# Scores on quarters of the TensorE array, transposes on the whole of it

## The chip, the cores and the metric

The kernel runs on one NeuronCore of a Trainium2 chip. The metric is the device time of one execution in microseconds; the kernel before takes 481.77 us (median of three runs, 481.53 to 481.87). In the profile PE is TensorE's matrix product, PEld its loading of weights, DVE is VectorE, ACT is ScalarE, POOL is GpSimd and SP is SyncE, which issues most transfers.

## What is computed

Two blocks follow each other. The first is a gated linear recurrence over 768 tokens for 4 batches x 8 heads, with a head of 48 values. For each token:

```
state = alpha[t][:, None] * state + outer(k[t], v[t])
y[t]  = q[t] @ state
```

The 8 heads of a token are put side by side into a row `x` of 384 values, 3072 rows in all. The second block is a feed-forward network without a nonlinearity: `((x @ w1) * (x @ w2)) @ w3 @ w_out`, with w1 and w2 of 384 x 1024, w3 of 1024 x 1024 and w_out of 1024 x 384. The weights arrive in double precision and are converted on the chip.

## The kernel before

**Part one, the recurrence, in 24 chunks.** A chunk is 128 tokens of one batch with all 8 heads; six chunks make up a batch. Inside a chunk the recurrence is turned into matrix products. `logs` and `decays` form the running product of the alphas (a logarithm, a triangular matmul, two exponentials) and `decayed` multiplies q and k by it, into `qk`, which has tokens on the partitions and each head padded from 48 to 64. Then four kinds of small products follow:

- `transposed(n)` (line 310) turns q and k of chunk n, so that the head's 48 values lie on partitions: two heads share the 128 partitions, the even one at 0 to 47 and the odd one at 64 to 111. ScalarE copies the two PSUM banks of results to `qkT` (line 312).
- `scores(n)` (line 350) multiplies k by q for each of the 8 heads, contracting over 48 values, to a 128 x 128 block. VectorE masks the two banks of results into `ms` (line 353).
- `attend_state(n)` (line 370) multiplies the state carried from the chunk before by q, and `attend(n)` (line 376) adds the masked scores times v. In the first chunk of a batch there is no state, and line 370 is left out.
- `outer(n)` (line 322) forms k times v, which VectorE and GpSimd add into the state. The last chunk of a batch leaves it out.

**Part two, the network.** Line 406 is the matmul of all its products, always the whole 128 x 128 array against 384 columns. The "gates" are the products with w1 and w2; part of them is handed out in pieces to the steps of part one, to fill TensorE. w3 and w_out are first multiplied with each other ("fold"), for which w3 is transposed on the whole array in line 508; at the end `project` multiplies the gates by the result.

**The order.** The loop at line 584 runs over n = 0 to 24, here called steps. A step loads inputs, then calls `attend_state(n - 1)`, `scores(n)`, `transposed(n + 1)`, `attend(n - 1)`, `outer(n)`, then pieces of gates and `decays(n + 3)` between them (line 275; line 272 in early chunks). `pieces` (line 598) is 0 up to step 6; after that every fourth step (10, 14, 18, 22) has none and the others have 3, 3 and 2. Before a step without pieces there is also a new group of x to be split in three (lines 398 to 400). Each engine works through its instructions in a fixed order that is settled when the kernel is built, and that follows this order of calls except for small exchanges. All PSUM tiles come from one pool of 8 banks, handed out in turn.

**How a small product lies on the array.** The partitions that its operands occupy choose the rows of the array, and the partitions of its result the columns. Before the change there are four shapes. Line 370 uses 64 x 64 quarters. Lines 350 and 310 use 64 rows x 128 columns, i.e. two halves. Lines 376 and 322 use 128 rows x 64 columns. The gates and line 275 use the whole array. An fp32 matmul appears in the profile as two instructions, a transpose as one.

Of the kernel before, what the change touches and what calls it, by code (L numbers as in the profile page):

```python
# [48 lines left out]
def kernel(  # L49
# [12 lines left out]
    nc = tc.nc  # L62
    B, H, S, D = q.shape
# [5 lines left out]
    NP = H // 2  # L69
    DP = 64  # L70
# [32 lines left out]
    def bank():  # L103
        return ps.tile([C, 512], FP32, tag="bank", name="bank")

    st, mark = {}, {}

    def after_marks(*names):
        stack = ExitStack()
        for x in names:  # L110
            stack.enter_context(tc.issue_after(mark[x]))
        return stack
# [16 lines left out]
    def load_a(n):  # L129
        if n < N:  # L130
            st["a", n] = inp.tile([C, H, D], FP32, tag="ac", name="ac")
            nc.sync.dma_start(out=st["a", n], in_=rows(alpha, n))

    def load_kq(n):
        if n >= N:
            return
        st["kq", n] = inp.tile([C, 2, H, D], FP32, tag="kq", name="kq")
        nc.sync.dma_start(out=st["kq", n][:, 0], in_=rows(k, n))
        nc.sync.dma_start(out=st["kq", n][:, 1], in_=rows(q, n))  # L139

    def load_v(n):
        if n < N:
            st["v", n] = vs[n % len(vs)]
            nc.sync.dma_start(out=st["v", n][:, :, 0:D], in_=rows(v, n))
# [10 lines left out]
    ident = const.tile([C, C], FP32, name="ident")  # L155
# [71 lines left out]
    def convert(steps, ahead=3):  # L227

        for _ in range(steps):
            fetch(ahead)  # L230
            if not begun:
                return
            x = begun.popleft()
            try:
                next(x)
                begun.appendleft(x)
            except StopIteration:
                pass
# [4 lines left out]
    def store():  # L243

        while later:
            dst, src = later.popleft()
            nc.sync.dma_start(out=dst, in_=src)

    def last(n):
        return n % NCH == NCH - 1  # L250

    def logs(n):
        if n >= N:
            return
        a = st.pop(("a", n)).rearrange("p h d -> p (h d)")
        la = st["la", n] = work.tile([C, DM], FP32, tag="la", name="la")
        nc.scalar.activation(la, a, AF.Ln)
        if n >= LATE:

            t = st["la", n] = work.tile([C, 2, DM], FP32R, tag="la2", name="la2", bufs=1)  # L260
            nc.scalar.copy(t[:, 0], la)
            nc.vector.tensor_sub(t[:, 1], la, t[:, 0].bitcast(FP32))
        if n in ends:
            nc.gpsimd.dma_start(out=ends[n][2:3], in_=a[0:1])
# [21 lines left out]
    def decayed(n):  # L286
        if n < N:
            mark["qk", n] = nc.vector.tensor_mul(qks[n % 3][:, :, :, 0:D], st.pop(("kq", n)),  # L288
                                 st.pop(("e", n)).rearrange("p i (h d) -> p i h d", h=H)).ins
# [9 lines left out]
    def transposed(n):  # L299
        if n >= N:  # L300
            return
        qk = qks[n % 3]
        qkT = work.tile([C, 2, NP, C], FP32, tag="qkT", name="qkT")

        tp = [bank().rearrange("p (i j c) -> p i j c", i=2, j=NP) for _ in range(2)]
        for i in range(2):
            for j in range(NP):
                for half in range(2):
                    s = ds(DP * half, DP)
                    nc.tensor.transpose(tp[half][:, i, j, :], qk[s, i, 2 * j:2 * j + 2, :], ident[s, s])  # L310
        for half in range(2):
            mark["qkT", n] = nc.scalar.copy(qkT[:, :, :, ds(DP * half, DP)], tp[half]).ins  # L312
        st["qkT", n] = qkT

    def outer(n):
        if n >= N or last(n):
            return
        qk, vc = qks[n % 3], st["v", n]
        s1 = bank()[:, 0:NP * D].rearrange("p (j d) -> p j d", j=NP)
        for j in range(NP):  # L320
            for i in range(2):
                nc.tensor.matmul(s1[ds(DP * i, DP), j, :], qk[:, 0, 2 * j + i, :], vc[:, 2 * j + i, 0:D],
                                 start=True, stop=True)

        if n % 2:
            to = st["T", n] = work.tile([C, NP, D], FP32, tag="tmp", name="tmp")
        else:
            to = Ts[1][:, :, 0:D]
        if n % NCH == 0:
            nc.vector.tensor_copy(out=to, in_=s1)  # L330
        else:
            nc.vector.tensor_add(to, s1, Ts[n % 2][:, :, 0:D])
# [11 lines left out]
    def scores(n):  # L344
        qkT = st["qkT", n]
        sc = [bank().rearrange("p (j c) -> p j c", j=NP) for _ in range(2)]
        for j in range(NP):
            for i in range(2):
                r = ds(DP * i, D)
                nc.tensor.matmul(sc[i][:, j, :], qkT[r, 0, j, :], qkT[r, 1, j, :], start=True, stop=True)  # L350
        ms = work.tile([C, 2, NP, C], FP32, tag="ms", name="ms")
        for i in range(2):
            masked = nc.vector.tensor_tensor(ms[:, i].bitcast(I32), sc[i].bitcast(I32), keep_bc, op=ALU.bitwise_and)  # L353
        ends_of_part1[0] = mark["ms", n] = masked.ins
        st["ms", n] = ms
# [3 lines left out]
    def attend_state(n):  # L359
        qkT = st.pop(("qkT", n))  # L360

        y = [bank()[:, 0:HP * C].rearrange("p (j c) -> p j c", c=C) for _ in range(2)]
        st["y", n] = y, [(half * HP + j, i, y[i][ds(DP * half, DP), j, :])
                         for j in range(HP) for i in range(2) for half in range(2)]
        if n % NCH:
            for j, i, to in st["y", n][1]:
                r = ds(DP * i, D)
                nc.tensor.matmul(to, Ts[n % 2][r, j, :], qkT[r, 1, j, :],  # L370
                                 start=(j % HP == 0), stop=False, skip_group_check=True)
# [22 lines left out]
    def split_x(g, i):  # L394
        x = st.pop(("xT", g))
        t = tr[i].tile([C, 3, KM, TG], FP32R, tag="x3", name="x3")
        st["x3", g] = t
        nc.scalar.activation(t[:, 0], x, AF.Copy, scale=1.0 - 2.0 ** -13)
        nc.vector.tensor_sub(t[:, 1], x, t[:, 0].bitcast(FP32))  # L399
        nc.vector.scalar_tensor_tensor(t[:, 2], t[:, 0].bitcast(FP32), -1.0 - 1.0 / P, x,  # L400
                                       op0=ALU.mult, op1=ALU.add)
# [73 lines left out]
    def gate(g, f):  # L475
        yield from (late_gate if late else early_gate)(g, f)
# [73 lines left out]
    def run(pieces):  # L550

        for _ in range(pieces):
            if not fill:
                return
            try:
                next(fill[0])
            except StopIteration:
                fill.popleft()
# [25 lines left out]
    for n in range(N + 1):  # L584
        store()
        load_v(n + AHEAD - 1)
        load_a(n + 5)
        load_kq(n + AHEAD)
        if n:
            attend_state(n - 1)  # L590
        if n < N:
            scores(n)
        transposed(n + 1)
        if n - 2 in begin:
            g, tiles = begin[n - 2]
            split_x(g, 0)
            fill.extend(gate(g, f) for f in tiles)
        pieces = (0, 3, 3, 2)[(n - 6) % 4] if n > 5 else 0
        if n == 0:
            with after_marks(("qkT", 0)):  # L600
                logs(2)
            decays(2)
            with after_marks(("e", 2)):
                logs(3)
        early = n < 7
        behind = after_marks(("qkT", n + 1), ("qk", n + 1)) if early else ExitStack()
        if n < N - 2:
            with behind:
                convert(2 if n == 0 else 1, 2 if n == 0 else 3)
        advance(n)  # L610
        if n:
            attend(n - 1)
        outer(n)
        run(pieces > 0)
        if early:
            with after_marks(("qkT", n + 1), ("qk", n + 1)):
                convert(1)
        with after_marks(*[("ms", n)] * (n < 3)):
            decayed(n + 2)
        logs(n + 4)  # L620
        if n in begin:
            load_x(begin[n][0])
        convert(early and n > 2)
        run(pieces > 1)
        decays(n + 3)
        if n < N - 2:
            convert(early or n % 3 == 0)
        run(pieces > 2)
        if n == N - 3:
            while begun:  # L630
                convert(1)
            weights.extend(load_out(j) for j in range(KF))
            fetch(4)
# [91 lines left out]
```

## Time and profile before

| Engine | Busy, us (share of 479.8 us) | Instructions |
|---|---|---|
| PE | 458.3 (96%) | 3824 |
| PEld | 434.4 (91%) | 3824 |
| DVE | 359.7 (75%) | 582 |
| ACT | 279.2 (58%) | 550 |
| POOL | 75.0 (16%) | 138 |

A busy share is a mean over stages. Part one lasts until about 190 us; after that PE runs matmuls of line 406 and the fold's transposes almost without a break. Since matmuls overlap each other, the mean duration of one (300 ns, say) is not what it costs. What it costs is the distance from one start to the next, and that is read from a timeline or from the chain of waits, where each piece covers only the time that it added.

### The profile page before, as it was taken

What the parts mean: (1) busy time and instruction counts of PE and PEld (TensorE: products, weight loads), DVE (VectorE), ACT (ScalarE), POOL (GpSimd) and SP (SyncE); (2) the same over time, 40 slices, a digit from 0 to 9 for tenths busy, and PEclk for the clock granted to TensorE, in tenths of its full rate; (3) what the DMA queues carried; (4) which work ended last, traced back from release to release, by engine and by line L of the source; (5) the groups of instructions that cost most, each with busy time, mean ns of one, the idle gap of its engine ahead of it and who ended that gap; (6) DMA issues with size and microseconds to landing.
All of it is one profiled execution on the core that took longest, in us unless ns stands there. A gap on an engine that the chain in (4) does not pass through costs nothing.

```text
span 479.8 us, 9999 instructions
## 1 busy us (share of the span) xinstructions
PE 458.3 (96%) x3824; PEld 434.4 (91%) x3824; DVE 359.7 (75%) x582; ACT 279.2 (58%) x550; POOL 75.0 (16%) x138
## 2 busy tenths in 40 slices
PE   4889889999998999999999999999999999999997
PEld 2576679899898998999999999999999999999996
DVE  2679999987989666999999788745541966667771
ACT  4566677766777454899777576545544533333330
POOL 2323132112201210112321112111111100000000
PEclk9998799999999999999999999999999999999999
DMA  9999999999999973557775443022104965556511
GB/s 157 192 198 203 219 216 192 219 210 216 214 215 226 217 222 110 190 158 246 227 215 188 135 159 100 34 100 83 49 34 132 258 193 167 169 172 179 180 51 49
DMA packets 155311, 80.29 MB, mean 167 GB/s; under 512 B 104672, under 2 KB 145760, under 8 KB 155264
## 3 DMA queue, kind: packets, MB, share of 16 engines
q1 hardware_dynamic: 149744, 65.23, 55.9%
q0 software_dynamic: 5520, 14.43, 9.2%
q8 instruction: 30, 0.49, 0.5%
q14 instruction: 17, 0.14, 0.1%
HBM read 57.58 MB, written 22.06 MB: 166 GB/s over the span
## 4 chain that ended last, share of the span: by engine, by line
PE 76%; DVE 8%; DMA 7%; ACT 3%; issue 3%; SPq 2%; ACTq 0%; DVEq 0%
PE bank L406 66%; DMA xT<-xd 2%; PE bank L376 2%; DMA raw<-in_moe_w_dram 2%; PE bank L350 2%; DMA ac<-in_alpha_dram 1%; PE bank L508 1%; PE bank L310 1%; DMA xd<-x 1%; DVE qk L288 1%; DVE ms L353 1%; PE bank L272 1%; DVE power L205 1%; DVE x L399 1%; SPq L139 1%
## 5 line engine op out<-in xcount | busy, mean ns | idle before, releaser
L406 PE MATMUL bank<-x,w 128*128 128x384 f32 x1152 | 211.2, 338 | 0.3 <-DVE x L400 0.3
L406 PEld LDWEIGHTS bank<-x,w 128*128 128x128 f32 x1152 | 200.1, 188 | 2.0 <-issue 1.3
L406 PE MATMUL bank<-w3o,ab 128*128 128x384 f32 x576 | 100.2, 336 | 0.0
L406 PEld LDWEIGHTS bank<-w3o,ab 128*128 128x128 f32 x576 | 99.9, 188 | 0.0
L431 ACT ACTIVATE bank<-bank 128x384 f32<-128x384 f32 x98 | 46.8, 477 | 42.7 <-PE bank L406 42.4
L415 ACT ACTIVATE t<-bank 128x384 f32<-128x384 f32 x62 | 30.4, 492 | 59.4 <-PE bank L406 59.1
L481 POOL DMA_DIRECT2D abd<-ab x46 | 27.5, 598 | 132.2 <-DVE ab L467 124.6
L467 DVE TENSOR_TENSOR ab<-bank,r 128x384 f32<-128x384 f32 x45 | 25.0, 555 | 22.7 <-ACT bank L431 17.7
L537 DVE TENSOR_TENSOR ab<-abl,ab 128x1024 fp32r<-128x1024 f32 x24 | 29.4, 1224 | 13.7 <-ACT ab L536 13.7
L536 ACT ACTIVATE ab<-abl 128x1024 fp32r<-128x1024 f32 x24 | 25.5, 1061 | 20.9 <-PE bank L406 18.9
L350 PEld LDWEIGHTS bank<-qkT 48*128 48x128 f32 x384 | 26.1, 204 | 10.8 <-issue 4.4
L406 PE MATMUL bank<-wo,w3T 128*128 128x384 f32 x192 | 35.9, 334 | 0.0
L350 PE MATMUL bank<-qkT 48*128 48x128 f32 x384 | 31.1, 304 | 3.7 <-DVE ms L353 2.4
L353 DVE TENSOR_TENSOR ms<-bank,keep 128x512 int32<-128x512 int32 x48 | 31.1, 686 | 4.2 <-PE bank L350 4.2
L406 PEld LDWEIGHTS bank<-wo,w3T 128*128 128x128 f32 x192 | 33.5, 188 | 0.0
L312 ACT COPY qkT<-bank 128x512 f32<-128x512 f32 x48 | 26.2, 591 | 11.0 <-PE bank L310 11.0
L417 DVE SCALAR_TENSOR_TENSOR o<-bank,t 128x384 f32<-128x384 f32 x24 | 13.4, 558 | 23.7 <-issue 15.2
L202 ACT ACTIVATE power<-power,rebias 128x512 uint32<-128x512 uint32 (+1 forms) x36 | 25.1, 699 | 9.0 <-DVE power L201 8.8
L197 ACT ACTIVATE rest<-raw 128x512 f32<-128x512 uint32 (+1 forms) x36 | 23.2, 647 | 12.0 <-DMA raw<-in_moe_w_dram 10.7
L288 DVE TENSOR_TENSOR qk<-kq,e 128x768 f32<-128x768 f32 x24 | 22.9, 954 | 8.9 <-ACT e L279 8.8
L538 DVE SCALAR_TENSOR_TENSOR ab<-ab,abl 128x1024 fp32r<-128x1024 f32 x24 | 29.2, 1219 | 0.0
L376 PE MATMUL bank<-ms,v 128*64 128x128 f32 x384 | 29.0, 294 | 0.0
(75 smaller groups left out, 571.6 us busy)
## 6 DMA issues: line engine op xcount, KB each, us to landing
abl<-abd SPq DMA_DIRECT2D x24, 512.0 KB, 4.5
abd<-ab POOLq DMA_DIRECT2D x46, 192.0 KB, 3.3
raw<-in_moe_w_dram SPq DMA_DIRECT2D x16, 512.0 KB, 5.1
raw<-in_moe_w_dram SPq DMA_DIRECT2D x24, 256.0 KB, 5.0
xT<-xd POOLq DMA_DIRECT2D x9, 576.0 KB, 4.6
ac<-in_alpha_dram SPq DMA_DIRECT2D x24, 192.0 KB, 5.3
kq<-in_k_dram SPq DMA_DIRECT2D x24, 192.0 KB, 5.3
kq<-in_q_dram SPq DMA_DIRECT2D x24, 192.0 KB, 4.3
```

Source lines behind the costliest of these rows:

```text
L288: mark["qk", n] = nc.vector.tensor_mul(qks[n % 3][:, :, :, 0:D], st.pop(("kq", n)), st.pop(("e", n)).rearrange("p i (h d) -> p i h d", h=H ...
L312: mark["qkT", n] = nc.scalar.copy(qkT[:, :, :, ds(DP * half, DP)], tp[half]).ins
L350: nc.tensor.matmul(sc[i][:, j, :], qkT[r, 0, j, :], qkT[r, 1, j, :], start=True, stop=True)
L353: masked = nc.vector.tensor_tensor(ms[:, i].bitcast(I32), sc[i].bitcast(I32), keep_bc, op=ALU.bitwise_and)
L376: nc.tensor.matmul(to, vc[:, 2 * j + i, :], ms[:, i, j, :], start=(n % NCH == 0 and j % HP == 0), stop=(j % HP == HP - 1), skip_group_chec ...
L406: nc.tensor.matmul(p, w[part][i], x[part][i], start=start and part == parts[0] and i == 0, stop=stop and part == parts[-1] and i == n - 1, ...
L415: nc.scalar.activation(t, p1, AF.Copy, scale=(1.0 + 1.0 / P) * scale)
L431: nc.scalar.activation(p, p, AF.Copy, scale=1.0 + 1.0 / P)
L481: (nc.gpsimd if late else nc.sync).dma_start(out=abd[g][:, f, :], in_=ab)
L536: nc.scalar.activation(t[:, 0], ab, AF.Copy, scale=1.0 - 2.0 ** -13)
L537: nc.vector.tensor_sub(t[:, 1], ab, t[:, 0].bitcast(FP32))
L538: nc.vector.scalar_tensor_tensor(t[:, 2], t[:, 0].bitcast(FP32), -1.0 - 1.0 / P, ab, op0=ALU.mult, op1=ALU.add)
```

## The change

Scores and transposes trade shapes. Each head's scores are split in two matmuls of 64 result rows each, so that they run on the quarters, as the state products just ahead of them do: 16 matmuls per chunk in place of 8. The transposes, 16 per chunk on 64 x 64 blocks before, become 8 on whole 128 x 128 blocks; ScalarE's two copies then take one bank for k and one for q, where each bank held one half of the tokens of both. In steps that have gates, the transposes move from behind the scores to behind the outer products, where the gates, also on the whole array, come next. The aim is fewer changes of shape on the array.

```
     def transposed(n):
-        tp = [bank().rearrange("p (i j c) -> p i j c", i=2, j=NP) for _ in range(2)]
         for i in range(2):
+            tp = bank().rearrange("p (j c) -> p j c", j=NP)
             for j in range(NP):
-                for half in range(2):
-                    s = ds(DP * half, DP)
-                    nc.tensor.transpose(tp[half][:, i, j, :], qk[s, i, 2 * j:2 * j + 2, :], ident[s, s])
-        for half in range(2):
-            mark["qkT", n] = nc.scalar.copy(qkT[:, :, :, ds(DP * half, DP)], tp[half]).ins
+                nc.tensor.transpose(tp[:, j, :], qk[:, i, 2 * j:2 * j + 2, :], ident)
+            mark["qkT", n] = nc.scalar.copy(qkT[:, i], tp).ins
...
     def scores(n):
         for j in range(NP):
             for i in range(2):
-                r = ds(DP * i, D)
-                nc.tensor.matmul(sc[i][:, j, :], qkT[r, 0, j, :], qkT[r, 1, j, :], start=True, stop=True)
+                for half in range(2):
+                    r, s = ds(DP * i, D), ds(DP * half, DP)
+                    nc.tensor.matmul(sc[i][s, j, :], qkT[r, 0, j, s], qkT[r, 1, j, :], start=True, stop=True)
...
             scores(n)
-        transposed(n + 1)
+        pieces = (0, 3, 3, 2)[(n - 6) % 4] if n > 5 else 0
+        if not pieces:
+            transposed(n + 1)
...
         outer(n)
+        if pieces:
+            transposed(n + 1)
         run(pieces > 0)
```

More of the change, by code (lines that the diff above doesn't have):

```diff
@@ L597 @@
             fill.extend(gate(g, f) for f in tiles)
-        pieces = (0, 3, 3, 2)[(n - 6) % 4] if n > 5 else 0
         if n == 0:
```

## The prediction

> **What bounds the kernel now.** I read the busy shares by slices first (40 slices of 12 us; digits are tenths).
>
> ```profile
> PE   4889889999998999999999999999999999999997
> ...
> DVE  2679999987989666999999788745541966667771
> ...
> PEclk9998799999999999999999999999999999999999
> DMA  9999999999999973557775443022104965556511
> ```
>
> PE is full from the seventh slice on. Before that VectorE and the transfers are as full as PE, and the clock dips. Next, what PE waits for between 65 and 190 us (in total, times, longest):
>
> ```profile
> PE bank L350 <- DVE ms L353: 1.7, 2, 1.3
> PE bank L275 <- ACT la L261: 1.0, 1, 1.0
> PE bank L310 <- ACT e L279: 0.7, 1, 0.7
> ```
>
> With two smaller rows (0.3 and 0.2) that is 3.9 us of 125. After 190 us there is no wait worth naming and nothing in the change. So from 65 us on the price of the change is PE time, less what those few waits can give back. Then the timeline of one step with gates (n = 16: start, length):
>
> ```profile
> 129.22 1.72 PE L406 MATMUL bank<-x,w 128*128 128x384 f32 x9
> 130.87 0.67 PE L370 MATMUL bank<-qkT,T 48*64 48x128 f32 x16
> 131.47 1.16 PE L350 MATMUL bank<-qkT 48*128 48x128 f32 x16
> 132.46 0.66 PE L310 MATMUL bank<-ident,qk 64*128 64x64 f32 x16
> 133.05 1.09 PE L376 MATMUL bank<-ms,v 128*64 128x128 f32 x16
> 133.97 0.62 PE L322 MATMUL bank<-v,qk 128*64 128x48 f32 x16
> ```
>
> The reader subtracts starts. State products take 0.60 us, scores 0.99, transposes 0.59, attends 0.92, and no group waits. These contain the cost of changing shape. Narrower windows give starts inside a group, and so the undisturbed spacing: state products start in fours 0.11 apart (131.03, 131.14), scores in pairs (131.68 for the second, so 0.78 / 7 = 0.11), transposes in pairs 0.06 apart. What exceeds that is the change of shape:
>
> - state to scores: the last four states start at 131.25, so the second pair of scores is due at 131.47 and starts at 131.68: **0.21 us**;
> - transposes to attends: second pair due at 133.06, starts at 133.21: **0.15**;
> - gates to state, read likewise: 0.15. Outer products to gates: second gate due at 134.60, starts at 134.81: **0.21**;
> - scores to transposes, and attends to outer, are of one shape: nothing;
> - state directly to attends, only in step 24 (188.59 for the last four, second pair due at 188.81, starts at 188.97): **0.16**.
>
> The row for a whole-array transpose is line 508; the chain of waits gives its net time, with gates around it:
>
> ```profile
> 253.83 0.87 PE bank L508 x8
> 254.71 13.53 PE bank L406 x78
> ```
>
> 0.87 / 8 = 0.109 us for one. Gates run at 13.53 / 78 = 0.173 behind them as everywhere, so whole-array transposes beside gates pay no change of shape.
>
> **What the Trainium skill says.** TensorEngine Tiling (Array Packing), Key Properties: changing the tiling mode, not only the tile, drains TensorE. The trace agrees: 0.15 to 0.21 us at each change and none within a mode. The same section says that different tiles load and multiply in parallel; the fours of line 370 start 7 ns or so apart within 0.03 us, so a quarter of the work per instruction is not a quarter of the speed. Restrictions on that page: column tiling excludes transpose mode for fp32. That is why the transposes cannot join the quarters and must take halves by rows or the whole array; no run so far shows it. TensorE: Matmul & The Clock Gate, Part 1: a little-used PE is put to half clock. The trace shows it early on: the stretch 51.7 to 58.5 us has a granted clock of 0.50.
>
> **The change part by part**, for a step in full clock.
>
> *Scores on quarters.* 32 passes in fours, 8 x 0.109 = 0.87 us, for 8 pairs, 8 x 0.111 = 0.89. Saves 0.02. No VectorE work changes: it masks the same two banks.
>
> *Transposes on the whole array.* 8 x 0.109 = 0.87 for 8 pairs x 0.062 = 0.50: **adds 0.37** in each chunk. The two 128 x 512 copies to `qkT` stay the same size (591 ns each in the groups view), and the first can begin when half the transposes are done; ScalarE has room (58% busy), so I cost it at nothing. Copies wait behind the later transposes in gated steps, but `qkT` is needed only in the next step, with 3 to 5 us of gates in between.
>
> *Changes of shape.* (a) Step with gates and state: before gates-state 0.15, state-scores 0.21, transposes-attends 0.15, outer-gates 0.21. After: gates-state 0.15, scores-attends 0.16 (as state-attends), outer-transposes 0.21 (as outer-gates), transposes-gates 0. Saves 0.20. (b) Step with gates, no state: there was no 0.21 in the middle to save; the first change falls from about 0.20 to 0.15: saves about 0.05. (c) Step without gates: the order stays, so quarters-transposes and transposes-attends replace 0.21 and 0.15. Neither is in the trace (quarters to whole, whole to column halves); bounded by 0 and 0.21 each, I take 0.36 for both, saving 0.
>
> *Sum from step 8 on.* (a) n = 8, 9, 11, 12, 15, 16, 17, 20, 21: 9 x (0.37 - 0.02 - 0.20) = 1.35. (b) 13, 19: 2 x 0.30 = 0.6. (c) 10, 14, 18, 22: 4 x 0.35 = 1.4 (-0.01 to 0.41 each). Step 23 has scores and no transposes: -0.02, -0.21, and scores-attends about as before: -0.25. Together **+3.1 us** of PE time, 1.7 to 3.3 with the bounds.
>
> *What waits give back.* Three waits stand before transposes that now move behind attends and outer products (0.9 to 1.5 us of work goes first): 0.7 in step 11, 0.2 in step 15, and in step 12 transposes that take 0.90 us in place of 0.59. That is 1.2; I count 1.1. The steps behind (c) open late because of something else. The chain of waits into step 19:
>
> ```profile
> 142.91 5.74 DMA xT<-xd
> ...
> 149.36 0.87 DVE qk L288
> 150.23 0.78 DVE x L399
> ...
> 151.41 0.70 DVE ms L353
> ...
> 152.24 1.16 PE bank L350 x16
> ```
>
> For 10 us it holds no PE work: a load of x, then VectorE's queue, in which the mask stands behind the split of x; PE's scores wait for it, and all of PE behind them. PE time added in step 18 is hidden under that 1.3 us. Step 11 likewise opens 0.5 late. Of the 1.4 us in (c) I count 0.9 as hidden. Remains 3.1 - 1.1 - 0.9 = **+1.1**.
>
> *The first 65 us.* Chunks 0 to 7: in half clock (0, 1, 2, 6) a transpose pair is 0.107 apart, so the whole-array form is estimated at 2 x 0.109 and costs 8 x 0.11 = +0.87; in full clock +0.37; steps 2 to 6 save 0.21 each. 4 x 0.87 + 4 x 0.37 - 5 x 0.21 = +3.9. Between 14 and 65 us, though, the chain of waits has 0.93 us of PE; it runs through VectorE's conversion of weights and three loads. VectorE waits for scores 3.0 us in that time, so PE is not wholly off the path. Before 14 us two groups of transposes are on the chain (1.12 and 1.11 us) and would add up to 1.7, but the built order also puts the logarithm of chunk 2 ahead of two exponentials on ScalarE, which frees the alpha load behind it sooner. I take +0.4 (-1 to +2).
>
> Sum: 1.1 + 0.4 = +1.5, so 481.77 + 1.5 = **483.3 us**.
>
> **The rivals.**
> - *All of it lands on the path.* PE is 96% busy and its waits may move rather than shrink: 3.1 + 1.7 = +4.8, 486.5 us. For it: n = 20, 21 and 16 have no wait at all. Against: the 10 us of chain without PE before step 19.
> - *Loads and VectorE set the end of part one.* The transfers' digits are 9 for 14 slices, VectorE is 19.8 of 20 us busy from 65 to 85. Then nearly all is absorbed: +0.2, 482.0 us.
> - *Faster.* The waits above, with those by which steps 11, 15 and 23 open late (about 0.4 each), come to 5 us; the built order also moves the masks ahead of the decayed q and k on VectorE in several steps. If these dissolve, 3.1 - 4.9 + 0.3 = -1.5, 480.3 us. Against: a wait on loads cannot vanish by a new order on PE, and ahead of the mask of step 18 the new order puts the split of x first, which may lengthen that wait.
>
> **How the numbers follow.** Forecast 0.44, all on the path 0.18, absorbed 0.20, faster 0.18. Slower by over 0.2% (0.96 us) takes the first two: 0.62; same 0.20; faster 0.18. The range leaves out about a tenth at each side: 480.5 to 486.0.
>
> **What would show it.** In a step with gates: scores follow the state products at 0.44 us (0.60 before); whole-array transposes take 0.87, and gates follow them at once; attends come 0.16 late. In a step without gates: the two unknown changes of shape, by starts. The stretch from step 8's first gate to the end of step 24 should be about 1 us longer, and the first gate of step 7 (63.41) less than 2 us later. The forecast is wrong if whole-array transposes run much faster than 0.11 us each, if the quarters of the scores don't overlap in fours, or if the clock dips of the first 60 us move.

## The result and the profile after

The changed kernel takes 483.87 us (median of six runs, 483.02 to 484.84) beside 481.65 us for the kernel before: a ratio of 1.006, with a 95% interval of 1.0032 to 1.0088. Run again later beside other kernels it gave 1.0040 (1.0022 to 1.0058). It is slower by about two microseconds.

First the same step of the timeline of the changed kernel, n = 16 (start, length; lines 368, 348, 374, 319, 308 and 404 are the old 370, 350, 376, 322, 310 and 406):

```profile
132.06 0.67 PE L368 MATMUL bank<-qkT,T 48*64 48x128 f32 x16
132.55 1.05 PE L348 MATMUL bank<-qkT 48*64 48x128 f32 x32
133.53 1.09 PE L374 MATMUL bank<-ms,v 128*64 128x128 f32 x16
134.46 0.62 PE L319 MATMUL bank<-v,qk 128*64 128x48 f32 x16
135.01 1.09 PE L308 MATMUL bank<-ident,qk 128*128 128x128 f32 x8
135.85 0.96 PE L404 MATMUL bank<-x,w 128*128 128x384 f32 x4
```

The reader subtracts starts again. Scores follow the state products after 0.49 us (0.60 before, 0.44 forecast), they take 0.98, and the transposes take 0.84 where they took 0.59 with the change of shape behind them included. The gates come at once: 135.85 is 0.03 behind the last transpose. A whole step, from one first state product to the next, grew from 8.90 us (130.87 to 139.76) to 9.06 (132.06 to 141.12).

Then a step without gates, n = 14, from the same timeline:

```profile
118.66 1.05 PE L348 MATMUL bank<-qkT 48*64 48x128 f32 x32
119.65 1.09 PE L308 MATMUL bank<-ident,qk 128*128 128x128 f32 x8
120.67 1.09 PE L374 MATMUL bank<-ms,v 128*64 128x128 f32 x16
121.59 0.62 PE L319 MATMUL bank<-v,qk 128*64 128x48 f32 x16
```

Transposes to attends is 1.02 us here, 0.59 in the step before the change; the step grew from 4.21 to 4.52.

What PE waits for between 65 and 190 us in the changed kernel (the view lists only waits of more than 0.15 us; in total, times, longest):

```profile
PE bank L275 <- ACT la L261: 1.0, 1, 1.0
PE bank L404 <- DVE x L397: 0.7, 1, 0.7
PE bank L404 <- DVE x L398: 0.6, 1, 0.6
PE bank L308 <- ACT x L378: 0.2, 1, 0.2
```

The waits of scores for a mask (1.7 us) and of transposes for an exponential (0.7) are gone. The first three rows all lie in step 7. From step 8 to the end of step 24 the view lists almost nothing.

The page's slices of the changed kernel show PE at 90% or more from the seventh of 40 slices to the last but one, with the granted clock in the top digit from the fifth on:

```profile
PE   4797689999999999999999999999999999999997
...
PEclk9798999999999999999999999999999999999999
```

Slices of 12 us are too coarse for two microseconds; they only say that no new hole has opened. The stretches of half clock in the first 65 us have moved, though, which the prediction named as a sign of being wrong: 41.4 to 44.8 and 51.7 to 58.5 us before, 18.3 to 25.1 and 42.2 to 45.6 after. Both pairs sum to 10.2 us, and the mean granted clock of the 18 later runs of the changed kernel (0.988) is not below that of the 51 runs of the kernel before beside them (0.985), so a lower clock does not explain the loss.

Two marks divide each profile, the start of step 8 and the end of step 24 (where the unbroken run of gates begins); the third figure is what lies between them. After the end of step 24 the kernels do the same work; it takes 289.9 us before and 290.1 after, with 291.0 in the second run of the changed kernel.

| Kernel | Step 8 starts, us | Step 24 ends, us | Between, us |
|---|---|---|---|
| before | 70.5 | 189.8 | 119.4 |
| changed | 71.8 | 191.4 | 119.6 |
| changed, second run | 70.2 | 190.0 | 119.8 |

So PE's waits pay for nearly all of what the change adds to steps 8 to 24. In the first pair most of the rest, 1.4 us, is there when step 8 starts; the second run shows that this mark scatters by more than that. Of the 1.2 us by which the profile of the second run is longer than that of the kernel before, 1.1 us lies after step 24, where the work is the same.

### The profile page after: what moved, and what is told of

It is laid out like the page before. It is cut to its first block, busy times and chain, and to the rows that moved or that the text cites. A ratio compares the mean times of both kernels' runs of the same rounds, so it can differ in the third digit from the quotient of the medians.

```text
span 481.5 us, 10389 instructions
## 1 busy us (share of the span) xinstructions
PE 458.8 (95%) x4016; PEld 434.5 (90%) x4016; DVE 360.4 (75%) x582; ACT 279.7 (58%) x550; POOL 75.0 (16%) x138
## 4 chain that ended last, share of the span: by engine, by line
PE 86%; DVE 5%; SPq 3%; ACT 2%; DMA 2%; issue 1%; DVEq 0%; ACTq 0%
PE bank L404 69%; PE bank L374 4%; PE bank L308 3%; PE bank L348 3%; PE bank L368 2%; PE bank L506 1%; DVE ms L351 1%; PE bank L319 1%; SPq L139 1%; PE bank L275 1%; DMA ac<-in_alpha_dram 1%; PE bank L272 1%; DMA raw<-in_moe_w_dram 1%; SPq L189 1%; DVE qk L288 1%
## 5 line engine op out<-in xcount | busy, mean ns | idle before, releaser
L308 PE MATMUL bank<-ident,qk 128*128 128x128 f32 x192 | 28.3, 295 | 6.4 <-DVE qk L288 6.3
L308 PEld LDWEIGHTS bank<-ident,qk 128*128 128x128 f32 x192 | 22.3, 149 | 10.7 <-issue 6.3
L415 DVE SCALAR_TENSOR_TENSOR r<-bank,t 128x384 f32<-128x384 f32 x38 | 21.1, 556 | 14.0 <-PE bank L404 8.2
```

The lines of the kernel that those rows point to most:

```text
L308: nc.tensor.transpose(tp[:, j, :], qk[:, i, 2 * j:2 * j + 2, :], ident)
L415: nc.vector.scalar_tensor_tensor(to, p2, scale, t, op0=ALU.mult, op1=ALU.add)
```

## The experiments

Ratios are to runs of the kernel before on the same chip, with 95% intervals. The marks come from one profile each. The first one scatters between 68 and 73 us over all these kernels: in step 4 alone PE's wait in front of the transposes, behind which a load stands, is between 0.0 and 2.9 us, and the stretches of half clock lie elsewhere in each profile. Ratios decide, marks explain. The built order of VectorE and ScalarE can also change when only TensorE's instructions are edited; it is the same in the two runs of the changed kernel and differs between the others.

**Scores alone on quarters.**

```
-                nc.tensor.matmul(sc[i][:, j, :], qkT[r, 0, j, :], qkT[r, 1, j, :], ...)
+                for half in range(2): nc.tensor.matmul(sc[i][s, j, :], qkT[r, 0, j, s], qkT[r, 1, j, :], ...)
```

> The scores alone on quarters; the transposes stay in halves by rows and in their old place. Theory (PE time by starts): the 0.21 us between state products and scores goes, but a new change of shape appears between scores and transposes (0.15 to 0.21), so a step gains 0.02 to 0.08 us and 17 such steps 0.3 to 1.3 us: 480.4 to 481.4 us. Rival (the quarters themselves save the changes of shape that they were made for): 16 times 0.21 = 3.4 us less, 478.3 us.

Measured: 1.0003 (0.9975 to 1.0031). The timeline of step 16 says why:

```profile
129.26 1.05 PE L351 MATMUL bank<-qkT 48*64 48x128 f32 x32
130.25 0.71 PE L310 MATMUL bank<-ident,qk 64*128 64x64 f32 x16
130.89 1.09 PE L377 MATMUL bank<-ms,v 128*64 128x128 f32 x16
```

State to scores is 0.49 us, but scores to transposes is no longer free: read by second starts, the change from quarters to halves costs 0.16. So 0.21 is exchanged for 0.16 and 0.02 is saved in the scores. The rival, 3.4 us faster or a ratio of 0.993, lies outside the interval; the gain that the theory gives, at most 0.3%, is too small to be told from none. The marks of this profile say little: step 8 starts at 68.4 us, the earliest of all, the stretch has a half-clock dip of 3.4 us at 153 us, and step 24 ends at 191.9.

**Transposes alone on the whole array, in their old place.** The edit is the first hunk of the change only.

> The transposes alone on the whole array, in their old place behind the scores; scores stay in halves. Theory: +0.37 us for each chunk's transposes and a new change of shape in front of them (0.15 to 0.21), so +0.55 in 15 steps of full clock, 8.2 us, less 1 to 2 us that waits give back, plus about 1.3 us in the first 65 us: 488 to 490 us. Rival (waits on loads and VectorE absorb PE time in part one): under 2 us more, below 483.7 us.

Measured: 1.0092 (1.0063 to 1.0121), 4.4 us, between the theory's 6 to 8 us and the rival's 2. The prices hold: 0.109 us each, and 0.153 for the change from halves to the whole array, which with 0.37 makes 0.52 in 15 steps, 7.8 us. The stretch from step 8 to step 24 grew only by 3.8 (119.4 to 123.2). From 72 to 190 us the waits of PE come down to one row:

```profile
PE bank L308 <- ACT e L279: 0.2, 1, 0.2
```

The theory underrated what waits give back: some 4 us. That is more than the 2.6 us of waits that the view lists for this stretch of the kernel before, so the rest must lie in pauses too short for its rows. Another 1.1 us of this profile's span came later, one wait for ScalarE at 380 us, with no counterpart before.

**Both new shapes, no move.** The two edits that move the transposes are left out.

> Both new shapes, but the transposes stay behind the scores in all steps. Theory: a step with gates has 0.67 us of changes of shape in place of 0.47 (entry 0.15, scores to transposes 0.17, transposes to attends 0.15, outer products to gates 0.21), so 11 steps cost 0.2 us more than in the changed kernel, 2.1 us, and the waits before the transposes of steps 11, 12 and 15 come back, up to 1.2 us: 485.8 to 487.3 us. Rival (the move is worth only its waits): 484.9 us. Rival (the move does nothing): 483.9 us.

Measured: 1.0078 (1.0049 to 1.0107), 3.8 us: just under the theory's 4.0 to 5.5, above the 3.1 and 2.1 of the two rivals, and with an interval (2.4 to 5.2 us) that rules out only the last of these. By second starts a gated step pays 0.145 at entry, 0.168 from scores to transposes, 0.144 from there to attends and 0.204 to the gates: 0.66, as expected. The interval touches that of the changed kernel, so the time alone does not settle the worth of the move; the starts do, 0.66 against 0.47 us a step.

**New from step 7 on, and new up to step 6.** Both make the two functions ask for the step number; the second has no move.

```
+        if n > 7:     # or n <= 7, in transposed(n); n > 6 or n <= 6 in scores(n)
```

> The old shapes and order up to step 6 (chunks 0 to 7 for the transposes), the new ones from step 7 on. Theory: the 1.2 to 1.4 us by which step 8 starts late come from the first steps (a weight load that lands later in VectorE's queue, and a state update ahead of the split of x), so they go and the rest stays: 482.3 to 482.7 us. Rival (the first 65 us differ by chance between runs, or the move in step 7 is to blame): 483.9 us.

> The counterpart of the kernel that changes from step 7 on: new shapes up to step 6 (chunks 0 to 7 for the transposes), the kernel before from there. Theory: most of the loss lies here. The changed kernel is 0.6% slower and the one that changes from step 7 on 0.06%, so this one should be 0.3 to 0.6% slower, 483.2 to 484.5 us when the kernel before takes 481.8. Rival (the loss needs both parts, or the first 65 us only scatter): within 0.2% of the kernel before.

Measured: 1.0006 (0.9988 to 1.0024) for the first, whose interval holds the +0.1 to +0.2% that was expected, but 0.9974 (0.9957 to 0.9991) for the second, which was expected to hold the loss and is faster than the kernel before. The theory that the loss lies in the first steps falls. Neither half loses alone; both together lose 0.4 to 0.6%. (The two halves ran on two chips and the second run of the changed kernel on a third, each beside the kernel before, so a difference between chips is not ruled out.) The marks:

| Kernel | Step 8 starts, us | Step 24 ends, us | Between, us |
|---|---|---|---|
| before | 70.5 | 189.8 | 119.4 |
| new up to step 6 | 73.1 | 190.6 | 117.6 |
| new from step 7 on | 70.1 | 189.6 | 119.5 |
| changed, two runs | 71.8 / 70.2 | 191.4 / 190.0 | 119.6 / 119.8 |

With the old shapes in the later steps, a step 8 that starts 2.6 us late finds shorter waits behind it (step 11 takes 8.89 us in place of 9.87, step 15 9.21 in place of 9.75), and part one ends 0.8 us late. With the new shapes the stretch is 119.5 to 119.8 us whether step 8 starts at 70.1 or 71.8: in these profiles a late start is passed on in full.

**New shapes only in steps with gates.**

```
+        if (0, 3, 3, 2)[(n - 6) % 4] > 0 and n > 5:   # scores; n - 1 for the transposes
```

> New shapes and the move only in steps with gates (7 to 9, 11 to 13, 15 to 17, 19 to 21, 23); in the first steps and in 10, 14, 18, 22 all as before. Theory: four steps of 0.31 us of PE time are saved against the kernel that changes from step 7 on, but what precedes step 11, 15, 19 and 23 is set by loads and VectorE, so at most half of the 1.2 us shows: 0 to 0.15% faster than the kernel before, 481.0 to 481.8 us. Rival (PE time counts in full): 1.2 us below the kernel that changes from step 7 on, 480.8 us. Rival (waits come back in full): no different from that kernel, 482.0 us.

Measured: 0.9993 (0.9970 to 1.0017). That agrees with the theory and is too close to both rivals to rule either out. Its stretch is 119.6 us, with step 8 at 72.7: again a late start that is passed on.

**The transposes in the rounded type.** Shortened to the lines that matter; the identity and the padding of q and k are also written by VectorE copies before the first chunk.

```
+    ident = const.tile([C, C], FP32R, ...)
+    qks = [p1.tile([C, 2, H, DP], FP32R, ...) ...]
...
+                nc.tensor.transpose(tp[:, j, :].bitcast(FP32R), qk[:, i, 2 * j:2 * j + 2, :], ident)
```

> The changed kernel with the operand of the transposes in the rounded fp32 type of the gates' parts: the decayed q and k and the identity are stored in that type[...]. Everything else, order and shapes, stays. Theory: a whole-array fp32 transpose takes 0.109 us[...]; in the rounded type [...]takes 0.055 to 0.075 us, so 8 take 0.45 to 0.6 in place of 0.87 and a step loses 0.3 to 0.4 us of PE time. Of the 5 us in all, waits on loads and VectorE give back about half: 480.5 to 482.5 us. Rival (the loading of 128 columns of weights sets the 0.109): no change in the spacing, 483.9 us.

Measured: 0.9997 (0.9978 to 1.0016), by the ratios 2 to 3 us below the changed kernel and in the middle of what was expected. The starts of step 16:

```profile
136.01 0.87 PE L312 MATMUL bank<-ident,qk 128*128 128x128 f32 x8
136.72 3.35 PE L408 MATMUL bank<-x,w 128*128 128x384 f32 x18
```

Eight transposes and their entry take 0.71 us, 0.84 before; inside the group they start 0.085 apart, not 0.109. That is less than the expected halving, and by second starts the gates behind them come 0.07 us late (0.01 before). The stretch from step 8 to 24 is 117.7 us, 1.9 below the changed kernel, with the same order of calls and the same shapes, though not the same built order. Of the 1.9 us, 0.9 lies in steps 18 and 19, where waits stand. So shorter transposes are enough to pay the loss back; that their duration is its cause is not shown, since the kernel that is new from step 7 on has the long ones and is not slower, and the changed kernel itself was not run on the chip of this experiment, on which none of the four kernels lost.

**Only the first transposes on the whole array** (chunks 0 to 7, nothing else).

> Only the transposes of chunks 0 to 7 on the whole array, in their old place; all scores in halves, all later transposes in halves. Theory: in the first steps the whole-array transposes are the longer PE work (0.87 in place of 0.50 us, twice that in half clock) and scores on quarters cost nothing, so this kernel shows all of the early loss: as slow as the one with both new shapes up to step 6, 0.3 to 0.6%. Rival (the build's new order on VectorE and ScalarE makes the early loss, whatever the shape): within 0.2% of the kernel before, or different from that kernel in either direction.

Measured: 0.9973 (0.9953 to 0.9993), again faster, which no theory had. Together with the kernel that is new up to step 6 it is the fastest seen, by 0.26%; both were measured on one chip against the same runs of the kernel before. Why is open: step 8 starts at 70.0 us here and at 73.1 there. Step 24 ends at 190.0 us here, at 190.6 there and at 189.8 in the kernel before: with the old shapes in the later steps the three end within 0.8 us of each other, though their starts lie 3.1 us apart (here a half-clock dip of 3.4 us at 152 us is in the stretch).

The last four test a new theory: part one has two budgets, one of loads and one of PE time.

**The changed kernel again.**

> The changed kernel once more, beside the next three on one chip. Theory (two budgets): part one ends at the later of two things, the loads with VectorE's queue behind them, or step 8's start plus the PE time of steps 8 to 24. The kernel before has some 4 us to spare in the second; the changed kernel spends about 2.3 on PE time and 1.4 on a late step 8 and is left with none. Then the loss seen first stands: 0.3 to 0.9% slower. Rival (the two halves, measured at +0.06% and -0.26%, simply add, and the first figure was a feature of that chip): within 0.3% of the kernel before.

Measured: 1.0040 (1.0022 to 1.0058). The loss stands, and as far as ratios from three chips can be compared the halves do not add.

**The changed kernel with old shapes in steps 10, 14, 18 and 22.**

> The changed kernel with the old shapes in the four steps without gates (10, 14, 18, 22). Theory: where PE has nothing to spare its time counts in full, so four times 0.31 us go: 1.0 to 1.3 us, 0.2 to 0.27%, below the changed kernel beside it. Rival (waits on loads set the end of part one here too, as between the kernels that change from step 7 on): no difference beyond 0.1%.

Measured: 1.0044 (1.0021 to 1.0067), no gain over the changed kernel. Of 1.24 us of PE time the stretch shows 0.4 to 0.6 (119.2 us), and a wait of 0.6 us is back at the head of step 11. The rival is nearer.

**More PE time in the kernel before, and in the changed one.** The added lines repeat transposes into the same place:

```
+        if n > 8:                      # before: 3 pairs, 0.19 us a step
+            for j in range(3):
+                for half in range(2):
+                    s = ds(DP * half, DP)
+                    nc.tensor.transpose(tp[half][:, 1, j, :], qk[s, 1, 2 * j:2 * j + 2, :], ident[s, s])
...
+            if n > 8 and i == 1:           # changed: 2 whole-array ones, 0.22 us a step
+                for j in range(2):
+                    nc.tensor.transpose(tp[:, j, :], qk[:, i, 2 * j:2 * j + 2, :], ident)
```

> The kernel before with six transposes of each chunk from 9 to 23 done twice (the same result into the same place): 3 pairs of 0.062 us in 15 steps, 2.8 us of PE time in the steps with waits, and nothing else changed. Theory: nearly 4 us of waits take it up: 0 to 0.15% slower, below 482.5 us when the kernel before takes 481.8. Rival (PE time counts in full): 0.58% slower, 484.6 us.

> The changed kernel with two whole-array transposes of each chunk from 9 to 23 done twice: 2 x 0.109 us in 15 steps, 3.3 us of PE time. Theory: no wait is left to take it up, so 2.8 to 3.3 us come on top of the changed kernel beside it, 0.58 to 0.68%. Rival (as in the kernel before, waits take it up): under 1 us on top.

Measured: 1.0073 (1.0047 to 1.0099) for the kernel before with 2.8 us more, and 1.0053 (1.0031 to 1.0074) for the changed one with 3.3 us more, which is 0.13% above the changed kernel beside it. Both went against the theory. In the first the stretch grew by 4.0 us (123.4), more than was added, and the waits between 72 and 190 us are as long as they were:

```profile
PE bank L355 <- DVE ms L358: 1.5, 1, 1.5
PE bank L375 <- DVE ms L358: 0.8, 2, 0.5
PE bank L310 <- DVE qk L288: 0.3, 1, 0.3
```

But the edit did more than add PE time: VectorE's built order changed with it. In the kernel before, the mask of step 18's scores, for which the scores of step 19 wait, stands between the two parts of the split of x that step 18 calls:

```profile
150.14 1.35 DVE L399 TENSOR_TENSOR x<-xT,x 128x1152 fp32r<-128x1152 f32 x1
151.41 1.28 DVE L353 TENSOR_TENSOR ms<-bank,keep 128x512 int32<-128x512 int32 x2
152.61 1.35 DVE L400 SCALAR_TENSOR_TENSOR x<-x,xT 128x1152 fp32r<-128x1152 f32 x1
```

Here it stands behind both, and step 19's scores wait 1.52 us for it:

```profile
151.62 1.36 DVE L404 TENSOR_TENSOR x<-xT,x 128x1152 fp32r<-128x1152 f32 x1 [1.18 <-ACT x L403]
152.90 0.55 DVE L262 TENSOR_TENSOR la<-la,la 128x384 fp32r<-128x384 f32 x1
153.37 1.35 DVE L405 SCALAR_TENSOR_TENSOR x<-x,xT 128x1152 fp32r<-128x1152 f32 x1
154.64 1.28 DVE L358 TENSOR_TENSOR ms<-bank,keep 128x512 int32<-128x512 int32 x2
```

In the kernel with the transposes alone on the whole array the added PE time has the same place, between scores and attends, but the mask (152.69) stands in front of both parts of the split (153.88 and 155.15); there some 4 of 7.8 us were taken up. So this experiment does not show that waits cannot take up PE time in that place; it shows that a build can renew a wait. In the second the stretch grew by 1.6 to 1.9 us (121.4), and no row of waits is left there. The changed kernel still had about 1.4 us to give, some 0.9 of it in pauses of 0.1 to 0.3 us among the gates of steps 9, 15 and 19 (the 18 first gates take 3.49, 3.56 and 3.56 us, and 3.21 in steps 11 and 13). The built order differs here too.

What survives of the two budgets is narrower: a late *start* of step 8 is forgiven with the old shapes and not with the new. What PE time added *inside* the steps costs depends on what the build does to the order of the other engines, and these two experiments do not separate the two.

## Why the prediction was right, and where its terms were off

**PE time per step: right.** Forecast +0.15, +0.30 and +0.35 us for the three kinds of step; measured in steps without waits +0.15 (8, 16, 17, 20; 0.10 in 21), +0.27 (13) and +0.31 (10, 14, 22). Sum 9 x 0.15 + 2 x 0.27 + 4 x 0.31 - 0.25 = 2.9, forecast 3.1.

**The unknown changes of shape.** Quarters to whole array: 0.167. Whole array to column halves: 0.145. Together 0.31, inside the bounds of 0 to 0.42, where 0.36 was taken. Scores to attends 0.16 and transposes to gates 0.01, as forecast. Outer products to transposes was forecast at 0.21 from the row of the gates and is 0.156. Eight transposes run at 0.109, as line 508 said.

**What waits give back: the sign right, the size short.** Steps 11, 12 and 15 became shorter by 0.89, 0.31 and 0.39 us, although PE works 0.15 us longer in each. Over steps 8 to 24 the stretch grew by 0.2 in the first pair and 0.4 in the second run, so waits gave back 2.5 to 2.7 of 2.9 where 2.0 was counted. The chain before step 19 was read rightly: steps 18 and 19 together take 13.84 us in place of 13.98, though PE works longer in them. The rival that put everything on the path (+4.8 us) is ruled out by the time. Within this stretch the result lies nearer to the rival that has nearly all absorbed (+0.2) than to the forecast's +1.1.

**The first 65 us: the wrong mechanism.** The forecast took +0.4 for longer transposes in half clock. In the first pair step 8 starts 1.4 us late. PE's transposes in step 4, before and after:

```profile
40.48 0.71 PE L310 MATMUL bank<-ident,qk 64*128 64x64 f32 x15 [0.23 <-ACT e L279]
...
41.69 1.50 PE L308 MATMUL bank<-ident,qk 128*128 128x128 f32 x8 [1.74 <-DVE qk L288]
```

VectorE's timeline shows what they wait for. Before:

```profile
38.64 0.35 DVE L332 TENSOR_TENSOR tmp<-bank,T 128x192 f32<-128x192 f32 x1
38.90 0.95 DVE L288 TENSOR_TENSOR qk<-kq,e 128x768 f32<-128x768 f32 x1
39.77 0.69 DVE L217 SCALAR_TENSOR_TENSOR w<-w,mant 128x512 fp32r<-128x512 f32 x1
```

After:

```profile
38.14 0.35 DVE L329 TENSOR_TENSOR tmp<-bank,T 128x192 f32<-128x192 f32 x1
39.38 0.69 DVE L217 SCALAR_TENSOR_TENSOR w<-w,mant 128x512 fp32r<-128x512 f32 x1 [0.89 <-ACT w L215]
...
40.59 0.95 DVE L288 TENSOR_TENSOR qk<-kq,e 128x768 f32<-128x768 f32 x1
```

VectorE is half a microsecond ahead until here. Then the built order has a weight's split, which waits through ScalarE for a load, in front of the decayed q and k. These start 1.7 us later than before, and PE's transposes wait 1.74 us for them. The order is the same in all seven profiles of kernels with both new shapes in these steps, and the wait there was between 0.0 and 2.9 us. The kernel with only the first transposes on the whole array has the order too and is not slower, nor is the one that is new up to step 6, with a wait of 2.3 us; so the order is a risk and not a fixed price. The forecast had read other parts of the new order, but not this one.

Step 7 adds a second piece. Its gates wait 0.7 and 0.6 us for the split of x, in both profiles of the changed kernel and in the one that is new from step 7 on; before, one wait of 0.30 stood there and 0.83 in front of the transposes. The first gate of step 7 starts at 63.56 us, only 0.15 later than before, as the prediction asked for; so in this pair 1.2 of the 1.4 us arise behind it, and most of step 4's delay had been made up. The kernel that is new from step 7 on has these waits and is not slower.

**The range** held the time, and "slower" was the likeliest case. The forecast of +1.5 came from +1.1 and +0.4; a measured +2.2 with +0.2 to +0.4 in steps 8 to 24 means that the two terms were each off, in opposite directions: that their sum came near is luck in part.

**What stays open.** How the two microseconds divide between step 4's wait, step 7's and the rest cannot be settled from single profiles, whose first mark scatters by as much. Taken together the profiles say a little more. In the seven profiles of kernels with both new shapes in the first steps, step 5 starts at 44.6 to 47.8 us (middle value 46.5) and step 8 at 70.2 to 73.1 (72.7); in the other seven, step 5 starts at 42.6 to 46.0 (43.7) and step 8 at 68.4 to 72.7 (70.5). A start that is later by about 2 us, forgiven where the old shapes follow and passed on where the new ones do, would give the loss and halves that do not add. This grouping was made after the fact from single profiles, and the experiments with added PE time are no test of it. One thing speaks against it: if the new shapes passed every late start on, the times of the changed kernel should scatter more than those of the kernel before, but its 18 later runs spread over 3.0 us and the 51 beside them over 6.6. So the account stays likely and not shown. The 0.26% that new shapes gain when they stop at step 6 is unexplained.

## What to carry to other kernels

A change of array shape has a price that can be read from second starts, and so has the work done in the new shape; here four changes became three and the saving was less than what the larger transposes cost. Before betting on a reordered engine, look in the built order for an instruction that waits on a load and has moved ahead of one that others wait for. Waits beside a full engine are not a stock that any added time may draw on: 2.9 us of added PE time were nearly all given back in one build, 7.8 us by half in a second, and 2.8 us not at all in a third. So before an experiment with added time is read, compare the built order of the other engines with the one it had without.

## What the runs showed of the hardware that was not expected

- Transposes of 128 x 128 values start every 0.085 us in the rounded fp32 type and every 0.109 in fp32: the rounded type saves about a fifth, far less than half.
- One and the same change of array shape differs in price with the products on its two sides: quarters to row halves costs 0.16 us from scores to transposes and 0.21 from state products to scores; column halves to whole array costs 0.156 in front of transposes and 0.21 in front of gates. The way back, whole array to column halves, costs 0.145.
- The half clock can come while PE is busy: in the stretch that the prediction names, 51.7 to 58.5 us of the kernel before, the granted clock is 0.50 and PE is busy 6.80 of 6.80 us; PE's one listed wait nearby, 2.2 us for a logarithm, lies before it, at about 48 to 50 us.
